# An adaLN, linear-attention and SwiGLU block on one core: a new order for the first scale block, and the output-projection fold in three batches

## The chip, the core and the metric

The kernel runs on one core of one Trainium2 chip. The core has five engines [...]: TensorE (PE, matmuls and 128x128 transposes; its weight loads are listed as PEld), VectorE (DVE), ScalarE (ACT), GpSimd (POOL) and SyncE (SP, which here only issues DMAs). DMAs issued from SP, ACT and POOL share 16 DMA engines. On-chip data lies in SBUF, matmul results in PSUM, which is used here as eight banks of 512 f32 columns: two pools, "pa" and "pb", of four banks each.

The metric is the device time of one execution, in microseconds, as the median over several runs. Before the change it is 829.95 us (8 runs, 829.49 to 830.62).

## The reference

x has 2048 rows of 1024 columns in bf16. Six vectors of 1024 come out of one small product with the condition c.

```python
mod = (silu(c) @ w_mod).reshape(1, 6, 1, -1)
sa, ca, ga, sb, cb, gb = mod[:, 0], ..., mod[:, 5]
h = layernorm(x) * (1 + ca) + sa
x = x + ga * A(h)                      # linear attention, 32 heads of 32
h = layernorm(x) * (1 + cb) + sb
x = x + gb * B(h)                      # (silu(h @ w_gate) * (h @ w_up)) @ w_down, F = 3584

# A(h): q, k, v = h @ wqkv; phi(t) = where(t > 0, t + 1, exp(t)) + 1e-6
kv  = sum_s phi(k)_s v_s               # 32 x 32 for each head
z   = sum_s phi(k)_s
o   = (phi(q) @ kv) / (phi(q) . z + 1e-6)
A   = o @ wo
```

## The kernel before

**Tiling.** The 2048 rows form four chunks (sc) of 512, each of four row tiles of 128. A 1024-wide contraction is eight blocks (cc) of 128. Almost every matmul is 128x128 weights times 512 columns into one PSUM bank. Big tiles (8 KB for each partition: weights, activations, phi(k), v, phi(q)) come from one pool of 19, called k8.

**Loads.** SP issues the first loads in the order of the program: x tiles 0 and 1, the eight blocks of w_mod's first scale columns (wca, 256 KB each; the first of them goes out from ACT), then wv's eight blocks with x tiles 2 and 3 among them, the eight blocks of the shift columns (wsa), the eight of wk, four more x tiles, and wq.

**The start (lines 454 to 529).** The instructions of DVE, ACT and POOL inside `in_order` keep the order in which they are written; PE keeps its program order everywhere. `keep_warm` and `keep_warm_f32` are matmuls on zeros whose result nobody reads. c is turned into a column layout and put through silu (scT). Row tiles 0 and 1 are normalised (xn), transposed on PE (`pe_transpose_tile`) and copied from PSUM to hT by DVE. `mod_rows` makes a row of the modulation on PE: for each of eight blocks j, four matmuls, each on a strip of 32 of the array's columns, stream 256 columns of weights. `mod_turn` then turns the row with a DVE transpose. For the very first column block, one more matmul for each j (`first`) gives the scale as a column right away. hs = hT times the scale; v of chunk 0 is computed from hs (`v_mms`), in groups of one PSUM bank each (row tile t, half nb of the columns), and the shift's part of v is added much later through a correction (vb, KVB). After v, the shift rows are made (`mod_rows(0, ...)`), hT gets scale and shift in place (`modulate_all`), and the k groups of chunk 0 begin, each of eight matmuls that need one wk block each.

**The middle.** For each later chunk: k groups, the kv sums of the chunk before (`kv_phase`: 128 matmuls of 64 columns on 32-column strips), v groups. phi takes an Exp on ACT and two DVE operations for each group. `mod_step` makes the other modulation vectors on DVE, with a broadcast row sc_row of silu(c), which the start builds with eight PE matmuls and two ACT copies. ga is multiplied into wo.

**The fold (lines 590 to 627).** After the last kv sums, kv is folded into wo, so that the attention output is one product of phi(q) with a folded wo. One unit of the fold is (h, nb, g): a PSUM bank that gets four matmuls, i = 0 to 3, each of 32x32 weights times 512 columns on the array tile of row group g and column group i.

```python
for i in range(HPC):
    for g in range(4):
        rs = slice(g * DH, (g + 1) * DH)
        mm(ps[g][i * DH:(i + 1) * DH, :], lhsT=KVT[rs, h, i * DH:(i + 1) * DH], rhs=wo[h][rs, i, ns], ...)
```

There are 16 units, in four batches of four, each batch on the four banks of "pb"; the results go back into wo in place, copied by ACT and DVE in turn. q groups of chunks 1 and 2 stand between the batches.

**The rest.** `wo_tile` applies the folded wo, adds x and normalises; `gate_up` and `down` are the SwiGLU part and take the time from about 200 us on.

Of the kernel before, what the change touches and what calls it, by code (L numbers as in the profile page):

```python
# [21 lines left out]
def kernel(  # L22
# [17 lines left out]
    DH = 32  # L40
# [62 lines left out]
    def big(name, shape):  # L103
        return k8.tile([P] + shape, BF16, name=name, tag="k8")
# [9 lines left out]
    c_sb = const.tile([DC, P], BF16, name="c_sb")  # L114

# [8 lines left out]
    for st in range(2):  # L124
        load_x(st, nc.sync)
# [3 lines left out]
    wca = [big("wme", [4, D]) for _ in range(2)]  # L129
# [6 lines left out]
    for j in range(DC):  # L136
        load_block(wca, wm_v, j, D, nc.scalar if j == 0 else nc.sync)
    for cc in range(DC):
        load_block(wv, wqkv_v, cc, 2 * D)
        if cc in (1, 4):  # L140
            load_x(2 + cc // 4, nc.sync)
# [26 lines left out]
    sc_row = const.tile([P, D], BF16, name="sc_row")  # L168
# [11 lines left out]
    sel = const.tile([P, HPC, P], BF16, name="sel")  # L180
# [17 lines left out]
    def bn(src, mv_out):  # L198
        stats = small.tile([P, NNB, nc.vector.BN_STATS_DIM], F32, name="stats")
        for i in range(NNB):  # L200
            nc.vector.bn_stats(out=stats[:, i, :], in_=src[:, i * NB:(i + 1) * NB])  # L201
        nc.vector.bn_aggr(out=mv_out, in_=stats[:])

    def normalise(dst, src, mean, rstd):
        nc.vector.tensor_scalar(out=dst, in0=src, scalar1=mean, scalar2=rstd, op0=ALU.subtract, op1=ALU.mult)

    def normalise_act(dst, src, mv, rstd):
        nmr = small.tile([P, 1], F32, name="nmr")
        last_nmr[0] = nc.gpsimd.tensor_scalar(out=nmr[:], in0=mv[:, 0, 0:1], scalar1=rstd[:, 0:1], scalar2=-1.0,  # L209
                                op0=ALU.mult, op1=ALU.mult)  # L210
        nc.scalar.activation(out=dst, in_=src, func=ACT.Identity, bias=nmr[:], scale=rstd[:, 0:1])  # L211
# [5 lines left out]
    def pe_transpose_tile(hT, xn, t):  # L217
        tp = acc_b("tp", (DC, P), BF16)
        for cc in range(DC):
            transpose(tp[:, cc, :], xn[:, cc * P:(cc + 1) * P])  # L220
        nc.vector.tensor_copy(out=hT[:, :, t * P:(t + 1) * P], in_=tp[:])
# [3 lines left out]
    def ln1_stats(sc, t):  # L225
        x_sb = x_tiles.pop(sc * STC + t)
        mv = small.tile([P, STC, 2], F32, name="mv")
        bn(x_sb, mv[:, 0, :])
        rstd = rstd_of(mv, 1)
        return sc, t, x_sb, mv, rstd  # L230

    def ln1_norm(sc, t, x_sb, mv, rstd, dve=False):
        xn = k2.tile([P, D], BF16, name="xn", bufs=4)
        if dve:
            normalise(xn[:], x_sb[:], mv[:, 0, 0:1], rstd[:, 0:1])
        else:
            normalise_act(xn[:], x_sb[:], mv, rstd)
        if sc > 0:
            last_load[0] = nc.sync.dma_start_transpose(hTs[sc][:, :, t * P:(t + 1) * P], xn[:])
        return xn  # L240
# [14 lines left out]
    def mod_rows(q, lo, hi, first=None):  # L255
        for j in range(lo, hi):
            if first is not None:
                mm(first, lhsT=wca[j // 4][:, j % 4, 0:P], rhs=scT[:, j:j + 1], start=False, stop=j == DC - 1)
            row_matvec(mod_ps[:, q * MW:(q + 1) * MW], sc32[:, j, :], (wsa, wca)[q][j // 4][:, j % 4, :],
                       q == 0 and j == 0, j == DC - 1)  # L260

    def mod_turn(lo, hi):
        nc.vector.transpose(out=scr_t[:, lo * DH:hi * DH], in_=mod_ps[:, lo * DH:hi * DH])

    def scale_to(hs, hT, cc, lo, hi):
        nc.vector.tensor_scalar(out=hs[:, cc, lo:hi], in0=hT[:, cc, lo:hi], scalar1=ca0T[:, cc:cc + 1], scalar2=None,
                                op0=ALU.mult)

# [185 lines left out]
    nc.vector.memset(sel[:], 0.0)  # L454

    def keep_warm(acc, n):
        for _ in range(n):
            mm(acc[:], lhsT=sel[:, 0, :], rhs=sel[:], start=True, stop=True)

    def keep_warm_f32(acc, n):  # L460
        zeros = sel[:].rearrange("p h n -> p (h n)").bitcast(F32)
        for _ in range(n):
            mm(acc[:, 0:zeros.shape[1]], lhsT=zeros[:, 0:P], rhs=zeros, start=True, stop=True)

    accs = [acc_a() for _ in range(4)]
    spare = accs[3]
    keep_warm_f32(spare, 3)
    keep_warm(spare, 1)
# [5 lines left out]
    with in_order(nc.vector, nc.scalar, nc.gpsimd):  # L474
        mod_ps = acc_b("mod_ps")
        mm(mod_ps[:, 0:DC], lhsT=c_sb[:], rhs=ident[0:DC, 0:DC], start=True, stop=True)
        for g in range(4):
            mm(mod_ps[g * DH:(g + 1) * DH, MW:2 * MW], lhsT=ident[:, 0:DH], rhs=base_t[:, 0:MW], start=True, stop=False)
        nc.scalar.activation(out=scT[:], in_=mod_ps[:, 0:DC], func=ACT.Silu)
        xn0 = ln1_norm(*ln1_stats(0, 0))  # L480
        st1 = ln1_stats(0, 1)
        nc.vector.tensor_copy(out=sc32[:], in_=scT[:].unsqueeze(2).to_broadcast([P, DC, DH]))
        xn1 = ln1_norm(*st1, dve=True)
        keep_warm_f32(spare, 1)
        for h in range(2):
            for j in range(DC // 2):
                mm(accs[h][:, j * P:(j + 1) * P], lhsT=scT[:, 4 * h + j:4 * h + j + 1].to_broadcast([P, P]), rhs=ident[:],
                   start=True, stop=True)
            nc.scalar.copy(out=sc_row[:, h * NB:(h + 1) * NB], in_=accs[h][:])
        keep_warm(spare, 3)  # L490
        first = accs[2][:, 0:1]
        mm(first, lhsT=ident[:], rhs=base_t[:, 0:1], start=True, stop=False)
        mod_rows(1, 0, 3, first)
        pe_transpose_tile(hT, xn0, 0)
        pe_transpose_tile(hT, xn1, 1)
        mod_rows(1, 3, DC, first)
        keep_warm(spare, 1)
        nc.vector.tensor_scalar(out=hs[:, 0, 0:H], in0=hT[:, 0, 0:H], scalar1=first, scalar2=None, op0=ALU.mult)
        mod_turn(DC, 2 * DC)
        for cc in range(1, 4):  # L500
            scale_to(hs, hT, cc, 0, H)
        xn2 = ln1_norm(*ln1_stats(0, 2))
        for cc in range(4, DC):
            scale_to(hs, hT, cc, 0, H)
        st3 = ln1_stats(0, 3)
        gs = k_groups[0:4]
        v_mms(hs, gs, accs, 0, 6)
        pe_transpose_tile(hT, xn2, 2)
        for cc in range(DC):
            scale_to(hs, hT, cc, H, H + P)  # L510
        xn3 = ln1_norm(*st3)
        v_mms(hs, gs, accs, 6, DC)
        gs2, accs2 = k_groups[4:6], [acc_b("acc") for _ in range(2)]
        v_mms(hs, gs2[0:1], accs2[0:1])
        v_evac(0, gs, accs)
        pe_transpose_tile(hT, xn3, 3)
        for cc in range(DC):
            scale_to(hs, hT, cc, H + P, SCW)
        v_mms(hs, gs2[1:2], accs2[1:2])
        mod_rows(0, 0, DC)  # L520
        mod_turn(0, DC)
        nc.vector.tensor_copy(out=sca[:], in_=scr[:, :, :, 0])
        v_evac(0, gs2, accs2)
        for g in k_groups[6:8]:
            acc = acc_a()
            v_mms(hs, [g], [acc])
            v_evac(0, [g], [acc])
        modulate_all(hT, ca1T, saT)
        nc.vector.tensor_copy(out=sc32[:], in_=saT.unsqueeze(2).to_broadcast([P, DC, DH]))
# [3 lines left out]
    for h in range(2):  # L533
        with tc.issue_after(last_load[0].ins):
            nc.sync.dma_start(out=wq[h][:], in_=wqkv_v[:, 4 * h:4 * h + 4, 0:D])
# [5 lines left out]
    for sc in range(NSC):  # L541
        if sc > 0:
            k_phase(sc, 0, 2)
            kv_phase(sc - 1)
            k_phase(sc, 2, 3)
# [45 lines left out]
    q_phase(1, 1, 2)  # L591
# [10 lines left out]
    def fold_wo(h, nb):  # L602
        ns = slice(nb * NB, (nb + 1) * NB)
        ps = [acc_b("wf") for _ in range(4)]
        for i in range(HPC):
            for g in range(4):
                rs = slice(g * DH, (g + 1) * DH)
                mm(ps[g][i * DH:(i + 1) * DH, :], lhsT=KVT[rs, h, i * DH:(i + 1) * DH], rhs=wo[h][rs, i, ns],
                   start=True, stop=True)
        for g in range(4):  # L610
            (nc.scalar.copy if g % 2 == 0 else nc.vector.tensor_copy)(out=wo[h][:, g, ns], in_=ps[g][:])

    q_phase(1, 2, 5)
# [5 lines left out]
    den_sum(0, acc_a())  # L619
    fold_wo(0, 0)  # L620
    den_spread(0)
    q_phase(1, 6, 8)
    fold_wo(0, 1)
    q_phase(2, 0, 2)
    fold_wo(1, 0)
    q_phase(2, 2, 4)
    fold_wo(1, 1)
# [3 lines left out]
    def wo_tile(st):  # L631
# [10 lines left out]
        for nb in range(NNB):  # L642
            ns = slice(nb * NB, (nb + 1) * NB)
            a_ps = acc_b("a_ps")
            for hg in range(HG):
                mm(a_ps[:], lhsT=pq[:, hg, t * P:(t + 1) * P], rhs=wo[hg // 4][:, hg % 4, ns],
                                 start=(hg == 0), stop=(hg == HG - 1))
# [144 lines left out]
```

## Time and profile before

| what | us |
|---|---|
| median of 8 runs | 829.95 |
| lowest and highest | 829.49, 830.62 |
| the profiled execution, its own time | 829.89 |
| span of its profile, first to last instruction | 828.1 |
| first useful matmul (acc<-wv) starts | 11.32 |
| first k group starts | 27.28 |
| fold, first batch to last | 154.82 to 166.96 |
| all HBM reads of the span | 101.98 MB |

The page of the profile gives, for the whole span, the busy time of each engine, the chain of work that ended last (followed back from the last instruction to whatever released each step) and the costliest groups of instructions. A group line reads: source line, engine, operation, output<-inputs, shapes, count, then busy time and mean duration. Nearly every PE instruction carries line 98 or 101, those of the two helpers `mm` and `transpose`, so PE's work is told apart by its tiles. The end of a matmul in the trace is modelled [...]; the pace of PE is read from starts. In the chain and in PE's timeline below, rows of equal instructions are merged.

### The profile page before, as it was taken

The numbers are of one execution on the slowest core, as the hardware profiler recorded it, in microseconds if no ns is written. First come the engines' busy times: TensorE is split into PE (matmuls) and PEld (weight loads), VectorE is DVE, ScalarE is ACT, GpSimd is POOL, SyncE is SP. The second block draws the span as 40 slices with busy tenths as digits, with TensorE's granted clock in tenths as the row PEclk, the third lists the DMA queues.
The fourth block names the chain that finished last, engine by engine and source line by source line (L and its number), as shares of the span: only waits on it lengthen the run. The fifth ranks groups of instructions, "written<-read, shape, count | busy, mean of one in ns | idle before, by whom it ended". The sixth has DMA issues, their size and how long they took to land.

```text
span 828.1 us, 11287 instructions
## 1 busy us (share of the span) xinstructions
PE 822.9 (99%) x4609; PEld 379.1 (46%) x4609; DVE 348.8 (42%) x680; ACT 168.0 (20%) x253; POOL 63.9 (8%) x165
## 2 busy tenths in 40 slices
PE   9999999999999999999999999999999999999998
PEld 5444444444444444444444444444444444444444
DVE  6869778886353344421111354222224432222222
ACT  3545343434111101101111010111111101111000
POOL 2101020120222002000000010000001100000000
PEclk9999999999999999999999999999999999999999
DMA  9978454139995836446252272753405629610011
GB/s 341 307 167 191 117 114 102 44 106 321 366 227 201 251 111 192 140 162 212 91 161 93 63 223 89 251 188 112 143 0 182 149 66 358 220 43 1 19 58 51
DMA packets 142212, 129.07 MB, mean 156 GB/s; under 512 B 58768, under 2 KB 120720, under 8 KB 141648
## 3 DMA queue, kind: packets, MB, share of 16 engines
q1 hardware_dynamic: 138208, 115.10, 46.4%
q0 software_dynamic: 3792, 12.98, 5.1%
q8 instruction: 36, 0.59, 0.3%
q10 hardware_dynamic: 160, 0.26, 0.1%
q14 instruction: 16, 0.13, 0.1%
HBM read 101.98 MB, written 12.72 MB: 138 GB/s over the span
## 4 chain that ended last, share of the span: by engine, by line
PE 98%; DMA 1%; DVE 0%; ACTq 0%; issue 0%
PE acc L98 90%; PE a_ps L98 7%; DMA wme<-in_w_mod_dram 1%; PE kvp L98 1%; PE wf L98 0%; PE den L98 0%; PE mod_ps L98 0%; PE tp L101 0%; PE vb L98 0%; ACTq L126 0%; DVE e L708 0%; DVE ob L711 0%
## 5 line engine op out<-in xcount | busy, mean ns | idle before, releaser
L98 PE MATMUL acc<-h2T,wgu 128*128 128x512 bf16 x1792 | 387.6, 379 | 0.0
L98 PEld LDWEIGHTS <-wgu 128*128 128x128 bf16 x1792 | 175.2, 98 | 211.3
L687 DVE TENSOR_TENSOR gu<-acc,e 128x512 bf16<-128x512 f32 x112 | 77.5, 692 | 289.9 <-PE acc L98 287.1
L98 PE MATMUL acc<-wd,gu 128*128 128x512 bf16 (+2 forms) x924 | 196.1, 373 | 0.0
L686 ACT ACTIVATE e<-acc 128x512 f32<-128x512 f32 x112 | 66.9, 597 | 374.8 <-PE acc L98 374.8
L98 PEld LDWEIGHTS <-gu 128*128 128x128 bf16 x924 | 89.3, 98 | 104.5
L708 DVE TENSOR_TENSOR e<-acc,gb_bc 128x512 f32<-128x512 f32 (+2 forms) x33 | 22.3, 675 | 131.7 <-PE acc L98 128.8
L98 PEld LDWEIGHTS <-hT 128*128 128x128 bf16 x448 | 43.6, 98 | 52.3
L98 PE MATMUL a_ps<-wo,pq 128*128 128x512 bf16 x256 | 57.4, 379 | 0.0
L98 PE MATMUL acc<-hT,wq 128*128 128x512 bf16 x256 | 56.7, 379 | 0.0
L98 PE MATMUL acc<-wk,hT 128*128 128x512 bf16 x256 | 56.4, 379 | 0.0
L273 ACT ACTIVATE eb<-acc 128x512 bf16<-128x512 f32 x64 | 37.6, 594 | 61.4 <-PE acc L98 59.2
L211 ACT ACTIVATE xn<-x,nmr,rstd 128x1024 bf16<-128x1024 f32 x16 | 19.8, 1240 | 126.2 <-POOL nmr L209 125.4
L98 PE MATMUL acc<-wv,hT 128*128 128x512 bf16 x192 | 41.9, 379 | 0.0
L98 PEld LDWEIGHTS <-pq 128*128 128x128 bf16 x256 | 25.1, 98 | 30.2
L655 POOL DMA_DIRECT2D x_scratch<-x x16 | 9.8, 615 | 373.7 <-DVE x L648 373.6
L98 PEld LDWEIGHTS <-wq 128*128 128x128 bf16 x256 | 24.6, 98 | 29.9 <-issue 1.1
L274 DVE TENSOR_SCALAR eb<-eb 128x512 bf16<-128x512 bf16 x64 | 18.3, 290 | 25.8 <-ACT eb L273 25.8
L648 DVE TENSOR_TENSOR x<-a_ps,x_sb 128x512 f32<-128x512 f32 x32 | 22.1, 691 | 8.6 <-PE a_ps L98 8.6
L195 POOL TENSOR_TENSOR rstd<-veps,neg_half 128x1 f32<-128x1 f32 x32 | 17.9, 561 | 99.0 <-DVE veps L193 86.7
L201 DVE BATCH_NORM_STATS2 stats<-x_sb 128x6 f32<-128x512 bf16 x32 | 20.9, 673 | 4.7 <-DMA x_sb<-in_A_x_dram 4.6
L711 DVE TENSOR_TENSOR ob<-e,x1r 128x512 bf16<-128x512 f32 (+2 forms) x33 | 22.3, 675 | 1.0
(99 smaller groups left out, 321.0 us busy)
## 6 DMA issues: line engine op xcount, KB each, us to landing
wgu<-in_B_w_gate_dram SPq DMA_DIRECT2D x28, 1024.0 KB, 6.8
wgu<-in_B_w_up_dram SPq DMA_DIRECT2D x28, 1024.0 KB, 8.0
x_sb<-in_A_x_dram SPq DMA_DIRECT2D x32, 256.0 KB, 5.3
x_scratch<-x POOLq DMA_DIRECT2D x16, 512.0 KB, 3.1
x1r<-x_scratch SPq DMA_DIRECT2D x31, 256.0 KB, 2.9
wd<-in_B_w_down_dram SPq DMA_DIRECT2D x7, 1024.0 KB, 6.8
rbc<-rden_scratch POOLq DMA_DIRECT2D x16, 256.0 KB, 7.6
out_dram<-ob SPq DMA_DIRECT2D x31, 128.0 KB, 1.7
```

What stands on the lines that cost most here:

```text
L98: return tc.keep_in_program_order(nc.tensor.matmul(out, lhsT=lhsT, rhs=rhs, start=start, stop=stop))
L195: nc.gpsimd.tensor_tensor(out=rstd[:, 0:n], in0=veps[:, 0:n], in1=neg_half[:].to_broadcast([P, n]), op=ALU.pow)
L201: nc.vector.bn_stats(out=stats[:, i, :], in_=src[:, i * NB:(i + 1) * NB])
L211: nc.scalar.activation(out=dst, in_=src, func=ACT.Identity, bias=nmr[:], scale=rstd[:, 0:1])
L273: nc.scalar.activation(out=e[:], in_=acc, func=ACT.Exp)
L274: nc.vector.tensor_scalar(out=e[:], in0=e[:], scalar1=1.0, scalar2=PHI_EPS, op0=ALU.min, op1=ALU.add)
L648: nc.vector.tensor_tensor(out=x1[:, ns], in0=a_ps[:], in1=x_t[:, ns], op=ALU.add)
L655: nc.gpsimd.dma_start(out=x1_dram[st * P:(st + 1) * P, :], in_=x1[:])
L686: nc.scalar.activation(out=sg[:], in_=ps[0][:], func=ACT.Silu)
L687: gm = nc.vector.tensor_tensor(out=guT[sc][f // GPT][:, f % GPT, :], in0=ps[1][:], in1=sg[:], op=ALU.mult)
L708: nc.vector.tensor_tensor(out=yt, in0=y_ps, in1=gb_bc[:, ns], op=ALU.mult)
L711: nc.vector.tensor_tensor(out=ob, in0=yt, in1=x1r, op=ALU.add)
```

## The change

At the start, the scale block is loaded in two halves of 512 columns (wca[h] is now [8 blocks, 512 columns], two blocks for each DMA, runs of 1 KB), half 0 ahead of wv and half 1 after wv's first four blocks; x tile 2 is loaded ahead of them. For half 0 the scale is made as four columns by matmuls that stream one column each (`ca_cols`), in four steps with no-op f32 matmuls between them. For half 1 it is made as a row as before, with 128 streamed columns for each matmul (`ca_rows`). Row tiles 0 and 1 are transposed in halves into two PSUM tiles; the first four blocks are scaled from there into hs by DVE, and ACT copies the PSUM tiles to hT. Tile 2's statistics are split around the normalisation of tile 1, which DVE and ACT share. Tile 2 (first four blocks) and tile 3 are scaled straight from PSUM. The v groups run over blocks 0 to 3 first, then 4 to 7. sc_row is no longer built by PE: c's row is loaded, put through silu by ACT, written to DRAM and read back as a broadcast.

Later, kv_phase comes one k group (or q group) earlier, and one q group of chunk 1 comes after it. The fold runs in batches of 5, 6 and 5 units, on "pb" and "pa" banks, into new tiles wof; the sums of den use a "pb" bank.

```diff
-    for st in range(2):
+    for st in range(3):
         load_x(st, nc.sync)
...
-    wca = [big("wme", [4, D]) for _ in range(2)]
+    wca = [big("wme", [DC, NB]) for _ in range(2)]
...
-    for j in range(DC):
-        load_block(wca, wm_v, j, D, nc.scalar if j == 0 else nc.sync)
-    for cc in range(DC):
+    def load_ca(h, eng0):
+        for k in range(4):
+            js = slice(2 * k, 2 * k + 2)
+            (eng0 if k == 0 else nc.sync).dma_start(out=wca[h][:, js, :], in_=wm_v[:, js, D + h * NB:D + (h + 1) * NB])
+
+    load_ca(0, nc.scalar)
+    nc.scalar.dma_start(out=sc_row[0:1, :], in_=c)
+    for cc in range(4):
         load_block(wv, wqkv_v, cc, 2 * D)
-        if cc in (1, 4):
-            load_x(2 + cc // 4, nc.sync)
+    load_ca(1, nc.sync)
+    load_x(3, nc.sync)
+    for cc in range(4, DC):
+        load_block(wv, wqkv_v, cc, 2 * D)
...
+    def ca_rows():
+        mod_rows(lambda j: wca[1][:, j, :], DC + 4, 4)
...
+    def scale_turned(tp, cc, t):
+        nc.vector.tensor_scalar(out=hs[:, cc, t * P:(t + 1) * P], in0=tp[:, cc, :], scalar1=ca0T[:, cc:cc + 1],
+                                scalar2=None, op0=ALU.mult)
...
+    def keep_warm(*widths):
+        for n in widths:
+            mm(accs[3][:, 0:n], lhsT=zeros[:, 0:P], rhs=zeros[:, 0:n], start=True, stop=True)
...
+        def ca_cols(k):
+            for i in range(4):
+                for j in (2 * k, 2 * k + 1):
+                    mm(cols[i], lhsT=wca[0][:, j, i * P:(i + 1) * P], rhs=scT[:, j:j + 1], start=False,
+                       stop=j == DC - 1 and i in (0, 3))
...
+        keep_warm(NB)
+        ca_cols(0)
+        keep_warm(NB, 2 * P)
+        ca_cols(1)
+        turn_half(xn0, 0, 0)
+        ca_cols(2)
+        keep_warm(P)
+        turn_half(xn0, 0, 1)
+        turn_half(xn1, 1, 0)
+        ca_cols(3)
+        keep_warm(P)
...
+        scale_first(0)
+        next(bn2)
+        rstd2 = rstd_of(mv2, 1)
+        for cc in range(1, 4):
+            scale_first(cc)
...
+        v_mms(hs, gs, accs, 0, 1)
+        turn_half(xn1, 1, 1)
+        nc.scalar.copy(out=hT[:, 4:8, 0:H], in_=tps[1][:])
+        nc.scalar.activation(out=sc_row[0:1, :], in_=sc_row[0:1, :], func=ACT.Silu)
+        v_mms(hs, gs, accs, 1, 3)
+        tp2 = turn_tile(xn2)
+        for cc in range(4):
+            scale_turned(tp2, cc, 2)
+        nc.scalar.copy(out=hT[:, :, H:H + P], in_=tp2[:])
+        v_mms(hs, gs, accs, 3, 4)
+        ca_rows()
+        mod_turn(DC + 4, 2 * DC)
...
+    nc.gpsimd.dma_start(out=sc_dram[:], in_=sc_row[0:1, :])
+    with tc.issue_after(wq_load.ins):
+        nc.sync.dma_start(out=sc_row[:], in_=sc_dram[:].to_broadcast([P, D]))
...
-            k_phase(sc, 0, 2)
+            k_phase(sc, 0, 1)
             kv_phase(sc - 1)
-            k_phase(sc, 2, 3)
+            k_phase(sc, 1, 3)
...
-    def fold_wo(h, nb):
-        ns = slice(nb * NB, (nb + 1) * NB)
-        ps = [acc_b("wf") for _ in range(4)]
+    wof = [big("wof", [4, D]) for _ in range(2)]
+    fold_units = [(h, nb, g) for h in range(2) for nb in range(NNB) for g in range(4)]
+
+    def fold_wo(accs):
+        units = [(fold_units.pop(0), acc) for acc in accs]
         for i in range(HPC):
-            for g in range(4):
+            for (h, nb, g), acc in units:
                 rs = slice(g * DH, (g + 1) * DH)
-                mm(ps[g][i * DH:(i + 1) * DH, :], lhsT=KVT[rs, h, i * DH:(i + 1) * DH], rhs=wo[h][rs, i, ns],
-                   start=True, stop=True)
-        for g in range(4):
-            (nc.scalar.copy if g % 2 == 0 else nc.vector.tensor_copy)(out=wo[h][:, g, ns], in_=ps[g][:])
-
-    q_phase(1, 2, 5)
+                mm(acc[i * DH:(i + 1) * DH, :], lhsT=KVT[rs, h, i * DH:(i + 1) * DH],
+                   rhs=wo[h][rs, i, nb * NB:(nb + 1) * NB], start=True, stop=True)
+        for k, ((h, nb, g), acc) in enumerate(units):
+            (nc.scalar.copy if k % 2 == 0 else nc.vector.tensor_copy)(out=wof[h][:, g, nb * NB:(nb + 1) * NB], in_=acc[:])
+
+    q_phase(1, 1, 5)
...
-    den_sum(0, acc_a())
-    fold_wo(0, 0)
+    den_sum(0)
+    fold_wo([acc_b("wf") for _ in range(3)] + [acc_a() for _ in range(2)])
     den_spread(0)
     q_phase(1, 6, 8)
-    fold_wo(0, 1)
-    q_phase(2, 0, 2)
-    fold_wo(1, 0)
-    q_phase(2, 2, 4)
-    fold_wo(1, 1)
+    q_phase(2, 0, 1)
+    fold_wo([acc_b("wf") for _ in range(4)] + [acc_a() for _ in range(2)])
+    q_phase(2, 1, 4)
+    fold_wo([acc_b("wf") for _ in range(4)] + [acc_a()])
```

## The prediction

> **What bounds the kernel now.** I read four views, in this order. First the page, for the engine that sets the end.
>
> ```profile
> PE 822.9 (99%) x4609; PEld 379.1 (46%) x4609; DVE 348.8 (42%) x680; ACT 168.0 (20%) x253; POOL 63.9 (8%) x165
> ...
> PE 98%; DMA 1%; DVE 0%; ACTq 0%; issue 0%
> ```
>
> TensorE (PE) is busy for 99% of the span and holds 98% of the chain that ended last. A microsecond is therefore gained or lost only where PE waits or streams something useless, or where its matmuls are fewer or come in a worse order. Next the chain of waits in the first 30 us (start, length, what).
>
> ```profile
> 1.33 3.58 DMA wme<-in_w_mod_dram
> 4.91 0.02 issue
> 4.92 5.55 DMA wme<-in_w_mod_dram
> 10.47 0.05 issue
> 10.52 0.18 PE acc L98
> 10.70 0.22 PE mod_ps L98 x4
> 10.92 0.32 PE acc L98
> 11.24 0.08 issue
> 11.32 1.89 PE acc L98 x8
> ```
>
> The first useful matmul starts at 11.32. It waits for the last of the ten 256 KB blocks (x tiles 0 and 1, eight of the scale block) that the transfers deliver by 10.47. From there on the chain is PE alone. This is the wait that the change attacks, so the next question is whether those transfers only come in the wrong order or are themselves the bound. For that I took busy time in two stretches (PE, PEld, DVE, ACT, POOL, granted clock, DMA share, GB/s) and the rows of the tile wk.
>
> ```profile
> 8.00:28.00 20.00, 19.70 (x162) 10.15 (x159) 14.76 (x49) 7.07 (x12) 3.32 (x39) 1.00 1.05 394
> 194.00:204.00 10.00, 10.00 (x48) 4.55 (x47) 7.81 (x19) 4.66 (x7) 0.00 (x0) 1.00 1.08 369
> ...
> L98 PE MATMUL acc<-wk,hT x36: 379/379/379, 27.3 to 34.8; 128*128 128x512 bf16 x36
> L134 SPq DMA_DIRECT2D wk<-in_A_wqkv_dram x8: 327/328/328, 18.5 to 23.3; - x8
> ...
> DMA to landing us min/median/max: 5.4/5.4/5.4
> ```
>
> From 8 to 28 us the DMA engines are full (share 1.05) at 394 GB/s. The last wk block is issued at 23.26 and lands 5.36 later, at 28.62. The first k group starts at 27.28 and its eighth matmul, which needs that block, comes seven spacings of 0.2157 us later, at 28.79. So the load stream is only 0.17 us ahead of PE at this point. Last, PE's timeline around the fold:
>
> ```profile
> 153.31 1.03 PE L98 MATMUL acc<-hT,wq 128*128 128x512 bf16 x4
> 154.26 0.63 PE L98 MATMUL acc<-pq,Zden 128*32 128x128 bf16 x32
> 154.82 0.43 PE L98 MATMUL wf<-wo,kvs 32*32 32x512 bf16 x16
> 155.19 3.63 PE L98 MATMUL acc<-hT,wq 128*128 128x512 bf16 x16
> 158.75 0.43 PE L98 MATMUL wf<-wo,kvs 32*32 32x512 bf16 x16
> 159.12 0.60 PE L98 MATMUL acc<-hT,wq 128*128 128x512 bf16 x2
> ```
>
> Sixteen fold matmuls, one on each 32x32 tile of the array, take 0.37 us from the first start to the next full-array start (154.82 to 155.19). A single one streams 512 columns, 0.213 us at the spacing above, so all sixteen run at once.
>
> [...] sixteen tiles overlap here; no run yet shows a matmul for a free tile held behind one for a busy tile. [...] from the last q matmul before a fold to the fold is 0.31 us against a spacing of 0.216, so 0.09 us. [...] The 256 KB blocks do land one after another, 0.66 us apart. [...] The f32 no-ops here are 0.427 us apart before 4.4 us and faster after it[...].
>
> **The change, part by part.**
>
> *Start.* The ten blocks before the first useful matmul become seven (x tiles 0 to 2, four of scale half 0), and wv's first block is the eighth. With 0.665 us a block, the seventh lands at 10.47 - 3 x 0.665 = 8.47. The scale halves move 1 KB runs instead of 2 KB. The second stretch above, mostly FFN weights in 1 KB runs, gives 369 GB/s against 394: 4 blocks cost 0.18 more, all eight 0.36. So scale half 0 is there at 8.65, the first hs piece (a 0.29 us DVE row, L498, now read from PSUM) near 9.3, wv's first block at 9.35, and the first useful matmul at about 9.4, 1.9 us earlier.
>
> *From there to the k groups.* PE owes 64 v matmuls (13.8 us), 20 transposes at 0.056 (1.1; it was 16 in the kernel before, whose other 16 came ahead of the start), the scale rows of half 1 (32 of 128 columns, about 0.65 with both mode changes) and the shift rows (1.0, the 0.99 of 22.90). Half 1 is the fifteenth block: 10.47 + 5 x 0.665 + 0.36 = 14.15. PE is at its rows after 16 matmuls and 12 transposes, 9.4 + 3.45 + 0.67 = 13.5, and waits 0.65. Sum: 9.4 + 13.8 + 1.1 + 0.65 + 1.0 + 0.65 = 26.6, against 27.28 before. The early start has shrunk to 0.7.
>
> *The k groups.* The transfers in front of the last wk block are the same blocks in another order, plus the 0.36 for the shorter runs; one 2 KB row of c is added on ACT's queue. So that block lands at 28.62 + 0.36 = 28.98, its matmul goes at 29.03, and the second group starts at 29.25. Before, it started at 27.28 + 8 x 0.2157 = 29.01. The whole start comes out at **+0.25 us**: PE reaches the k groups earlier and waits for wk there. Bounds: the 1 KB price may be nothing, and an instruction fetch (36 packets, 0.59 MB on the page, so 16 KB each) [...] can move by its own length, near 0.8 us (SP's longest wait for wv). That gives -0.4, where PE's own 26.6 + 1.73 rules again, to +0.7. Work moved to ACT (hT copies, scale copies) and DVE (scaling from PSUM) lies beside those matmuls. If it slipped, it would first use up the 0.6 us that PE waits for wk.
>
> *No-ops.* sel's five f32 and bf16 groups give way to f32 ones of 512, 256 and 128 columns between the steps. They run while PE waits for blocks: nothing. [...]
>
> *kv one group earlier, q tile 1 later, sc_row by a DMA round trip.* The same matmuls and mode changes in another order. v's last copy ends 0.6 us after its matmul and kv still has a k group (1.73 us) of cover. sc_row's read-back stands on SP behind wq and ahead of the hT transposes, which are needed only near 57 us: nothing.
>
> *Fold.* Before: 4 batches x 0.37 plus 4 mode changes x 0.09 = 1.84 us. After: batches of 5, 6 and 5 units. A unit is four matmuls, i = 0..3, on tiles (g, i), and the loop has i outside and units inside. In each batch two units share a g. For every i the fifth matmul therefore meets a tile that is still streaming, waits 0.213, and holds everything behind it. First to last start is 3 x 0.22 + 0.216 = 0.87 instead of 0.05, so a batch takes 0.37 + 0.82 = 1.19. Three of them plus 3 x 0.09 = 3.84 us, **+2.0 us**. Bounds: if a held matmul let those for other tiles pass, a tile would have two turns per batch, 0.58 a batch and 2.0 in all, +0.2. [...] 12 x 0.09 more, +3.1. I take +2.0, [...] because matmuls that follow each other on the same tile keep one stream length apart: den's 96, four tiles of 128 columns at a time, take 1.45 us of the chain, 0.060 for each four, where 128 columns stream in 0.054. The copies to wof (16 of 0.6 to 0.68 us, as before) stay beside q matmuls; the two "pa" accumulators per batch come back before q needs them, three groups later. Every later stage is PE without gaps, so this reaches the end.
>
> Sum: +0.25 + 2.0 = +2.25 us on the profiled execution's span of 828.1. Its own time is 829.89 (1.8 around the span, untouched), and the median of the runs 829.95 is 0.06 above it. Forecast: **832.2 us**.
>
> **Rivals.**
> A. Forecast as above, 832.2, chance 0.72.
> B. Tiles dispatch independently: the fold costs +0.2, total +0.45, 830.4. For: tiles overlap freely at 0.003 us in the trace. [...] 0.13.
> C. Not slower but faster: the start's 1.9 us reach the end, the wk stream running ahead as soon as PE's order allows, and the fold as in B: 829.95 - 1.9 + 0.2 = 828.3. It decides if the last wk block lands before 27.1 instead of 29.0. Against: the full DMA share from 8 to 28 us, and PE's own sum of 26.6. 0.07.
> D. Slower still: [...] near 833.3. 0.08.
>
> **How the numbers follow.** The likeliest is A. The range 830.2 to 833.4 takes in B, D and A with the start at either bound (831.5 to 832.7); only C lies outside. What a measurement can tell from no change is about 0.2%, 1.66 us. A is beyond that unless the start is at its best bound, so slower is 0.67 of A's 0.72 plus D, 0.75. Same is B plus the rest of A, 0.18. Faster is C, 0.07.
>
> **What would show it.** Start: first acc<-wv near 9.4, a PE wait of 0.5 to 0.8 us for wme near 13.5, first acc<-wk near 26.6 with a wait for wk in it, second k group at 29.2 or 29.3. Fold: three wf batches of about 1.2 us each. The prediction is wrong if a batch takes 0.6 or less, or if the second k group starts before 28.5.

## The result, and the profile after

The changed kernel takes 833.18 us (median of 10 runs, 831.94 to 834.77), the kernel before beside it 829.89: ratio 1.0040, 95% interval 1.0032 to 1.0048. That is about 3.3 us slower, where the forecast was 2.25 us slower. The profiled execution took 834.58 with a span of 832.8, so 4.7 us more than the 828.1 of the kernel before. The page, for the engine that sets the end:

```profile
PE 824.9 (99%) x4623; PEld 378.9 (46%) x4623; DVE 347.0 (42%) x684; ACT 173.7 (21%) x261; POOL 65.1 (8%) x167
...
PE 96%; DMA 3%; issue 0%; SPq 0%; DVE 0%
```

TensorE still sets the end, and its share of the chain fell from 98 to 96% because the chain now runs through transfers for longer at the start. The chain of waits of the changed kernel, its end within the first 40 us (start, length, what):

```profile
23.66 5.36 DMA wk<-in_A_wqkv_dram
29.02 0.04 issue
29.06 10.95 PE acc L98 x50
```

The last wk block lands at 29.02 (forecast 28.98) and its matmul goes at 29.06, so the second k group starts one spacing of 0.216 later, near 29.27 (forecast 29.25, before 29.01). The start does what the forecast said. Next the fold, on the timeline of PE:

```profile
159.48 0.39 PE L98 MATMUL wf<-wo,kvs 32*32 32x512 bf16 x3
159.49 0.38 PE L98 MATMUL acc<-wo,kvs 32*32 32x512 bf16 x1
159.50 0.39 PE L98 MATMUL wf<-wo,kvs 32*32 32x512 bf16 x3
159.51 0.39 PE L98 MATMUL acc<-wo,kvs 32*32 32x512 bf16 x1
159.51 0.39 PE L98 MATMUL wf<-wo,kvs 32*32 32x512 bf16 x3
159.53 0.38 PE L98 MATMUL acc<-wo,kvs 32*32 32x512 bf16 x1
159.53 0.39 PE L98 MATMUL wf<-wo,kvs 32*32 32x512 bf16 x3
159.54 0.59 PE L98 MATMUL acc<-wo,kvs 32*32 32x512 bf16 x5
160.06 5.35 PE L98 MATMUL acc<-hT,wq 128*128 128x512 bf16 x24
```

In the program, each step i has five matmuls: three on wf, two on acc, of which the second acc one needs the tile that the first wf one occupies. Yet after one acc matmul the next step's wf matmuls start at once. The four that conflict come at the end, inside the last row with its five. A batch takes 0.58 us from first start to the next q matmul, not the 1.19 of the forecast. So the forecast's main term did not occur. What did is in the chain of the changed kernel from 50 to 70 us, a place that the forecast had passed over:

```profile
49.94 7.12 PE acc L98 x33
57.06 1.15 PE kvp L98 x128
58.21 1.19 PE acc L98 x5
59.40 2.54 issue
61.94 8.11 PE acc L98 x29
```

"issue" means that PE waits for nothing that the profile shows. It stands still for 2.54 us in the middle of a k group, and no operand is named as missing. Busy times around it (start:end, length, then PE, PEld, DVE, ACT, POOL, granted clock, DMA share, GB/s):

```profile
59.40:61.94 2.54, 0.00 (x0) 0.00 (x0) 0.00 (x0) 0.00 (x0) 0.00 (x0) 1.00 0.08 17
...
62.91:66.32 3.41, 3.41 (x10) 1.21 (x8) 0.98 (x2) 0.87 (x2) 0.00 (x0) 0.50 0.03 5
66.32:70.00 3.68, 3.68 (x18) 1.67 (x17) 3.38 (x9) 1.14 (x3) 0.00 (x0) 1.00 0.23 53
```

All five stand still at once, and 0.97 us after PE resumes the granted clock falls to 0.50 for 3.41 us. Half of 3.41 makes another 1.7 us, an estimate. The 2.54 count from a modelled end; by starts (59.02 to 61.94, less one spacing) PE loses 2.70. The sum closes nearly: second k group +0.26, stall 2.70, clock 1.7, fold 0.2 make 4.9, against 4.7 between the two spans and 4.85 between the starts of the last matmul.

What does PE wait for? The page of either kernel has 36 packets of 16 KB on a queue called "instruction". PE's 4609 matmuls and 4609 weight loads on the page make 256 for each packet, the 4623 of each in the changed kernel 257. In the records, fetches come on average 254.5 and 253.0 PE instructions apart. So a block, as the text below calls it, is one packet of about 256 PE instructions, an estimate from these counts. Two stretches of the changed kernel's DMA queues (queue, kind: packets, MB, and the time of the packets as a share of 16 engines, which can pass 100% where packets overlap), 54.0 to 59.4 and then 59.4 to 60.6:

```profile
q1 hardware_dynamic: 5576, 1.42, 116.2%
```

```profile
q1 hardware_dynamic: 129, 0.03, 10.9%
q8 instruction: 1, 0.02, 5.5%
```

Before 59.4 the DMA engines are full (116.2%), with w_mod's transposing loads (wmt). The fetch starts only at 59.46, when these run out; PE goes on 2.48 us later. In the kernel before, the fetch starts at 57.87, just as the same loads run out there, and PE is not yet dry. Its queues from 57.8 to 59.0:

```profile
q8 instruction: 1, 0.02, 5.0%
q1 hardware_dynamic: 22, 0.00, 1.7%
```

The loads run later in the changed kernel because SP issues them later. SP's timeline of the kernel before, then of the changed one (the starts count; the merged last row ends with the view):

```profile
34.31 9.50 SPq L239 DMA_TRANSPOSE hT<-xn  x4
43.91 1.96 SPq L121 DMA_DIRECT2D x_sb<-in_A_x_dram  x4
45.92 21.41 SPq L380 DMA_TRANSPOSE wmt<-in_w_mod_dram  x3
```

```profile
36.28 9.76 SPq L247 DMA_TRANSPOSE hT<-xn  x4
46.14 1.96 SPq L123 DMA_DIRECT2D x_sb<-in_A_x_dram  x4
48.15 9.88 SPq L392 DMA_TRANSPOSE wmt<-in_w_mod_dram  x2
```

The hT transposes start 2 us later and push the x loads and wmt by 2.2. They wait for chunk 1's xn, whose first tile ACT starts at 35.02 instead of 33.05. On DVE the modulation of chunk 0, now 16 half rows, ends at 29.8 instead of 27.3. Before, DVE then waited for x until 29.34, so chunk 1's statistics start only 0.58 later, at 29.92. The larger part comes next: the phi work of the first two k groups (31.11 to 33.3) now runs ahead of the step that sums up the first tile's statistics, at 33.23 instead of 31.14.

This is the theory (T) that the runs had to test. PE's next block of instructions is itself a DMA, and behind queued loads it comes late. A rival (R) puts the loss into the new scale block or its order on DVE. T needs a second piece: kv_phase is 128 matmuls and 128 weight loads, by the estimate above a whole block, that PE uses up in 1.15 us, where 128 full-size matmuls take 27.6 (at 0.216). Around kv_phase, T says, PE therefore has almost no stock to wait with.

### The profile page after: what moved, and what is told of

The parts are those of the page before. It is cut to its first block, busy times and chain, and to the rows that moved or that the text cites. A ratio compares the mean times of both kernels' runs of the same rounds, so it can differ in the third digit from the quotient of the medians.

```text
span 832.8 us, 11335 instructions
## 1 busy us (share of the span) xinstructions
PE 824.9 (99%) x4623; PEld 378.9 (46%) x4623; DVE 347.0 (42%) x684; ACT 173.7 (21%) x261; POOL 65.1 (8%) x167
## 4 chain that ended last, share of the span: by engine, by line
PE 96%; DMA 3%; issue 0%; SPq 0%; DVE 0%
PE acc L98 88%; PE a_ps L98 7%; DMA wme<-in_w_mod_dram 1%; DMA wv<-in_A_wqkv_dram 1%; DMA wk<-in_A_wqkv_dram 1%; DMA x_sb<-in_A_x_dram 1%; PE kvp L98 1%; PE den L98 0%; PE wf L98 0%; PE vb L98 0%; SPq L123 0%; DVE e L757 0%; DVE ob L760 0%; PE tp L101 0%
## 5 line engine op out<-in xcount | busy, mean ns | idle before, releaser
L98 PE MATMUL acc<-wk,hT 128*128 128x512 bf16 x256 | 58.7, 387 | 3.1 <-issue 2.5
L98 PE MATMUL a_ps<-wof,pq 128*128 128x512 bf16 x256 | 57.4, 379 | 0.0
L221 ACT ACTIVATE xn<-x_sb,nmr,rstd 128x1024 bf16<-128x1024 bf16 (+1 forms) x17 | 19.6, 1163 | 15.3 <-POOL nmr L216 12.2
```

What stands on the lines that cost most here:

```text
L98: return tc.keep_in_program_order(nc.tensor.matmul(out, lhsT=lhsT, rhs=rhs, start=start, stop=stop))
L221: nc.scalar.activation(out=dst[:, ws], in_=src[:, ws], func=ACT.Identity, bias=nmr[:], scale=rstd[:, 0:1])
```

## The experiments

The numbers give the order of the runs, and each ratio is to the kernel before as it ran beside them: a median of 830.11 for e1 to e4, 829.99 for e5 to e8, 830.14 for e9 and e10, 829.98 for e11 and e12.

### One part of the change alone

**e2_before_kv_early**: the kernel before with only kv_phase moved.

```diff
-            k_phase(sc, 0, 2)
+            k_phase(sc, 0, 1)
             kv_phase(sc - 1)
-            k_phase(sc, 2, 3)
+            k_phase(sc, 1, 3)
```

(and q tile 1 behind kv, as in the change).

> The kernel before with nothing changed but kv_phase one group earlier. T: the transposing loads end at 57.8 as in the kernel before, instructions come at about 60.3, PE's stock ends near 59.2: a stall of about 1.1 us, 831.0. R2: the stall of the changed kernel, 2.7 us and perhaps a clock dip: 832.5 or more. If the fetch has nothing to do with it: 829.9.

830.20, ratio 1.0003 (0.9995 to 1.0011). The move costs nothing by itself. T had said 831.0, a miss: the loads ran out at 56.8 and not at 57.8, the fetch started there, at 56.84, and PE had no gap but one of 0.16 us behind kvp.

**e3_before_fold3**: the kernel before with only the fold in three batches of 5, 6 and 5 units.

```diff
-    fold_wo(0, 0)
+    fold_wo([acc_b("wf") for _ in range(3)] + [acc_a() for _ in range(2)])
...
-    fold_wo(0, 1)
-    q_phase(2, 0, 2)
-    fold_wo(1, 0)
-    q_phase(2, 2, 4)
-    fold_wo(1, 1)
+    q_phase(2, 0, 1)
+    fold_wo([acc_b("wf") for _ in range(4)] + [acc_a() for _ in range(2)])
+    q_phase(2, 1, 4)
+    fold_wo([acc_b("wf") for _ in range(4)] + [acc_a()])
```

> The kernel before with the fold alone in three batches of 5, 6 and 5 units into wof. As recorded in the forecast (a held matmul holds all behind it): batches of 1.2 us, 831.9. Rival, each tile takes its next matmul when it is free: batches of 0.58 us, 830.1.

830.48, ratio 1.0006 (0.9997 to 1.0014). Its second batch on PE's timeline:

```profile
161.08 0.46 PE L98 MATMUL wf<-wo,kvs 32*32 32x512 bf16 x16
161.30 0.44 PE L98 MATMUL acc<-wo,kvs 32*32 32x512 bf16 x8
161.67 5.35 PE L98 MATMUL acc<-hT,wq 128*128 128x512 bf16 x23
```

From 161.08 to 161.67 it takes 0.59 us. The interval leaves no room for +2.0 us (0.24%): the fold's forecast term falls.

### One part of the change undone

**e1_after_kv_back**: the changed kernel with kv_phase back behind two k groups.

```diff
-            k_phase(sc, 0, 1)
+            k_phase(sc, 0, 2)
             kv_phase(sc - 1)
-            k_phase(sc, 1, 3)
+            k_phase(sc, 2, 3)
```

(and q tile 1 ahead of the last kv sums, as in the kernel before).

> The changed kernel with kv_phase moved back behind two k (or q) groups; head and fold as changed. Theory T: PE's instruction list is itself fetched by a DMA, the fetch that is wanted near 57 us is held until the transposing loads of w_mod (wmt) are through at about 59.4, and PE gets its next instructions some 2.5 us after that, near 61.9. With kv back, PE's stock would last to about 59.9, so a stall of about 2 us remains: 832 to 833.5. Rival R2, the move of kv alone makes PE outrun its instructions: the stall is gone, 830.2 to 830.6. Rival F, the fold costs 2 us by itself: without the stall 832.2.

831.93, ratio 1.0028 (1.0019 to 1.0037), just under T's 832 to 833.5. Its chain of waits:

```profile
58.67 1.20 PE kvp L98 x125
59.86 1.17 issue
61.03 0.21 PE kvp L98 x3
```

The stall is there, 1.17 instead of 2.54, and now inside kvp, three matmuls before its end. In the changed kernel PE got five k matmuls beyond kvp. Moving kv back put eight matmuls of a k group ahead of it, and eight is the shift: PE stops at the same place in its list of instructions, not at the same piece of work. That speaks for the end of a block. The fetch started at 58.53, and PE resumed 2.50 later. It did not wait for the loads to end, though: they ran at a DMA share of 1.27 just before it (57.5 to 58.5) and went on until 61.5; a lull lay about 2 us back.

**e4_after_turned_first**: the changed kernel with the transposing loads ahead of the x loads of chunk 2.

```diff
+        if sc == 0:
+            with tc.issue_after(last_load[0].ins):
+                last_load[0] = mod_load(2, gaT)
         if sc + 2 < NSC:
             for st in range((sc + 2) * STC, (sc + 3) * STC):
```

> The changed kernel with the transposing loads of w_mod's columns for gaT issued ahead of the four x tiles of chunk 2 instead of behind them. T: they are through about 2 us earlier, near 57.4, instructions come near 59.9, PE's stock ends at 59.2: a stall of about 0.7 us and no clock dip, 831.0. R2: stall and dip as before this edit, 832 to 834.8.

831.90, ratio 1.0025 (1.0015 to 1.0036); T had said 831.0. The transposing loads are through near 56.3, but the fetch starts at 59.12, when most of the x loads behind them are through. So it isn't the transposing alone: here the fetch came late behind ordinary loads, with the queue of loads at 95.0% of the 16 engines from 56.3 to 59.0. The chain:

```profile
58.80 1.03 PE acc L98 x4
59.82 1.58 issue
61.40 8.79 PE acc L98 x40
```

### The instructions shifted against the work

If the end of a block is what matters, then instructions without use, put into PE's idle time of the start, must move the stall.

**e8_after_80_more** and **e10_after_80_dense**: the changed kernel with 40 matmuls (80 instructions with their weight loads) in place of one of the no-ops; of one column in e8, of 64 in e10.

```diff
-        keep_warm(NB, 2 * P)
+        keep_warm(2 * P)
+        for _ in range(40):
+            mm(accs[3][:, 0:64], lhsT=ident[:], rhs=ident[:, 0:64], start=True, stop=True)
```

> The changed kernel with 40 one-column matmuls (80 PE instructions) in place of one of the start's idle-time matmuls of 0.93 us. T: the fetch that was late is asked for 80 instructions earlier, near 45 us, when no long loads are queued, and the following one is asked for inside kvp with a whole block in hand: no stall near 59 us, 830.4 to 830.6, that is, more instructions make it faster. R: 833.2 as without them.

830.35, ratio 1.0011 (1.0004 to 1.0017). In its profile, of an execution of 832.4, there was no stall near 59 us, but PE's records were long from 4.8 us on, ahead of the added matmuls, until 13.9 (the two no-ops at 4.8 span 2.06 us, in the changed kernel 1.14), and the first useful matmul came at 12.1. Six of the 21 runs lie at 832.4 to 832.6. Whether matmuls of one column prolong the slow start isn't shown; e10 took 64 columns instead:

> As e8_after_80_more, but each of the 40 added matmuls has 64 columns instead of one, so that PE is not thinly used in the idle time of the start (in the profile of e8_after_80_more the first useful matmul came at 12.1 us instead of 9.6 and the records were longer up to there). T: the start is as in the changed kernel (first useful matmul near 9.6, second k group near 29.3), the fetch is asked for near 45 to 50 us, no stall near 59 us: 830.4 with a span near 828.6. R: the stall near 59 us stays, 832 to 834.8.

830.38, ratio 1.0005 (0.9997 to 1.0013), span 828.4. The chain of e10, and its fetch in the stretch from 47.3 to 48.5:

```profile
49.94 7.12 PE acc L98 x33
57.06 1.15 PE kvp L98 x128
58.21 11.98 PE acc L98 x55
```

```profile
q1 hardware_dynamic: 139, 0.24, 65.0%
q8 instruction: 1, 0.02, 12.6%
```

From 49.94 to 58.21 this is the changed kernel to the hundredth. But by T PE has the block already, fetched at 47.34 between two groups of loads, and nothing stops. Chunk 1's first v matmul starts at 70.24 instead of 74.64: the 4.40 are the 2.70 of the stall and the 1.70 of the clock. The 40 useless matmuls make the changed kernel 2.8 us faster (833.18 against 830.38; the kernel before ran at 829.89 and 830.14 beside them). With the no-op gone the trace has 38 weight loads more, so 76 instructions. The scale block and its order on DVE are unchanged, so R has nothing left to explain.

### The loads moved, or the cause put into the kernel before

**e6_after_late_turn**: the changed kernel with the transposing loads behind kv_phase(0).

```diff
             if sc == 1:
+                mod_load(2, gaT, True)
                 mod_load(3, sbT, True)
...
-        if sc == 0:
-            with tc.issue_after(last_load[0].ins):
-                last_load[0] = mod_load(2, gaT)
```

> The changed kernel with the two transposing loads of w_mod for gaT issued in chunk 1 behind kv_phase(0) instead of at the end of chunk 0. T: no load is queued when PE wants its next instructions (about 55 to 57 us), so the fetch starts there, no stall near 59 us and no clock drop behind it; what remains of the change is the start's +0.25 and the fold's +0.2: 830.4 to 830.6. R: the stall near 59 us stays, 832 to 834.8.

837.45, ratio 1.0088 (1.0075 to 1.0102): a miss in the time. With no load under way the fetch started at 56.74, against 59.46 in the changed kernel, whose PE has as many instructions ahead of that place, and the stall near 59 us was gone, as T said. But the late loads pushed chunk 2's hT transposes behind them on SP, and PE stood still for 4.04 us until 88.47. The chain:

```profile
84.76 3.12 DMA hT<-xn
...
88.00 0.42 DVE hT L224
88.43 0.05 issue
88.47 3.58 PE acc L98 x8
```

**e5_before_pad** and **e9_before_pad_behind**: the kernel before with an unread 1 MB load, ahead of the two transposing loads in e5, behind them in e9.

```diff
+            pad = big("pad", [4, D])
+            with tc.issue_after(last_load[0].ins):
+                last_load[0] = nc.sync.dma_start(out=pad[:], in_=wqkv_v[:, 0:4, 0:D])
```

> The kernel before with one extra 1 MB load that nobody reads, queued between the x loads of chunk 2 and the two transposing loads of w_mod, so that the queue of loads empties about 2.6 us later (it was at 57.9 us). Theory T (PE's next 16 KB of instructions is itself a DMA that waits behind the loads already queued; PE resumes 2.5 us after the fetch starts): PE wants the block from about 57 us, the fetch starts near 60.4 instead of 57.87, PE can go on near 62.9, while its stock ends near 61.2 (kvp's end at 59.6 and some 7 matmuls); a stall of about 1.7 us, near 831.8. Rival R (the loss of the changed kernel comes from its new scale block or its order on DVE, not from instruction supply): no stall near 60 us, 830.1.

830.25, ratio 1.0004 (0.9996 to 1.0012): a miss. The fetch started at 59.07, early enough. The expectation for e9 below puts that into a gap between the two transposing loads. The trace has this gap at 56.4 to 57.0 (DMA share 0.17); at 58.5 to 59.0 the share is 1.22 again, so the fetch came in about 2 us behind the gap, with the second load in full stream.

> The kernel before with the extra 1 MB load that nobody reads queued behind the two transposing loads of w_mod, so that no gap is left between them in which PE's instructions could slip through, as they did at 59.07 us in e5_before_pad. T: the fetch wanted near 57 us starts when the pad is nearly through, 59.5 to 60.4 us; PE can go on 2.4 us later, at 62 to 62.8; its stock ends some 8 matmuls behind kvp, near 61.3: a stall of 0.7 to 1.5 us near 61 us, 830.7 to 831.6. Rival R (instruction supply plays no part): no stall, 830.0.

830.05, ratio 0.9998 (0.9990 to 1.0007). PE's timeline of e9, and its queues in the stretches from 57.2 to 60.4 and from 60.4 to 61.4:

```profile
58.73 1.22 PE L98 MATMUL kvp<-v,pk 128*32 128x64 bf16 x128
59.88 2.55 PE L98 MATMUL acc<-wk,hT 128*128 128x512 bf16 x11
62.86 4.49 PE L98 MATMUL acc<-wk,hT 128*128 128x512 bf16 x20 [0.43 <-issue]
```

```profile
q1 hardware_dynamic: 498, 0.99, 87.1%
```

```profile
q8 instruction: 1, 0.02, 6.0%
q1 hardware_dynamic: 2, 0.00, 0.1%
```

The fetch started at 60.44, with the pad through, and PE resumed 2.42 later. So the kernel before has the same stall once its loads last longer. It is 0.43 us instead of the expected 0.7 to 1.5, since PE got 11 matmuls beyond kvp and not 8. That is too little for the timed runs to show: their 830.05 is what R said, and the stall is seen in the profile alone.

**e7_before_32_more**, **e11_before_46_more**, **e12_before_46_more_and_pad**: the kernel before with more instructions at the start: 16 one-column matmuls in e7 (32 instructions), the edit below in e11 and e12 (46 by my count; the trace has 21 weight loads more, so 42), and in e12 e9's pad as well.

```diff
-    keep_warm_f32(spare, 3)
-    keep_warm(spare, 1)
+    keep_warm_f32(spare, 2)
+    for _ in range(24):
+        mm(spare[:, 0:64], lhsT=sel[:, 0, :], rhs=sel[:, 0, 0:64], start=True, stop=True)
```

> The kernel before with 16 more one-column matmuls (32 PE instructions with their weight loads, about 0.4 us) in PE's idle time before c arrives at 4.48 us. T: the block of instructions that PE lacks begins 32 instructions earlier against the work, in the last part of kvp: PE's stock ends near 59.5 instead of 61.2, the fetch still starts at 57.9 and PE resumes near 60.4: a stall of about 0.9 us, 831.0. R: 830.1.

> The kernel before with 24 matmuls of 64 columns in PE's idle time of the start, in place of two of the matmuls without use there: 46 PE instructions more ahead of kvp, PE as busy as before in that time. In e9_before_pad_behind the stock ended 11 matmuls behind kvp, near 62.3; with 46 instructions more it ends inside kvp, near 59.5. T: the fetch starts when the transposing loads are through, at 56.8 to 57.9, and PE can go on at 59.2 to 60.3: no stall or one of up to 0.8 us, 830.1 to 830.9. R: 830.1.

> Both additions to the kernel before at once: the 46 PE instructions of e11_before_46_more and the unread 1 MB load behind the transposing loads of e9_before_pad_behind, which cost nothing measurable each by itself. T: the stock ends near 59.5 inside kvp, the fetch starts near 60.4 behind the pad and PE goes on near 62.8: a stall of about 3.3 us inside kvp, and perhaps the drop of the granted clock behind it (1.7 us more): 833.4 to 835.2. R (the two are independent and instruction supply plays no part): 830.1 to 830.3.

831.00 (ratio 1.0010, 1.0003 to 1.0017), 830.62 (1.0008, 1.0000 to 1.0016) and 830.46 (1.0005, 0.9997 to 1.0014). e7 gave the expected time for another reason: no stall, but the k groups started 1.1 us later. In e11 and e12 the fetch started as early as 53.25 and 54.11: in e11 in the lull between the two transposing loads, in e12 about 1 us behind it, with the second one in full stream (share 1.27 from 53.5 to 54.1). So a stall of over 3 us, put into the kernel before, was not achieved. That an early request escapes agrees with T, but e12's time lies nearer to R's 830.1 to 830.3 than to T's 833.4 and shows nothing against R.

## Why the prediction was right and wrong

The direction and the range held, the mechanism did not: the largest term did not come, and a somewhat larger loss, from steps that the prediction had put at nothing, stood in its place. Step by step:

**Start: right.** First useful matmul at 9.60 (forecast 9.4), first k group at 26.53 (26.6), last wk block at 29.02 (28.98), second k group at 29.27 (29.25): +0.26 for +0.25. The early start is eaten by the load stream, as worked out. One term on the way did not come: PE did not wait 0.65 for the second scale half. Its rows began at 13.82, 0.31 behind the matmul before, the same step as at 23.8 (0.31). So 26.53 fits 26.6 in part by luck; the last wk block, which sets the end of this stretch, does not depend on it.

**Fold: wrong, +0.2 instead of +2.0.** The step "waits 0.213, and holds everything behind it" (the measured spacing is 0.216) failed in its second half. In the records of the batch above a matmul for a busy tile held only its own tile: sixteen matmuls start between 159.48 and 159.54 and the four that conflict at 159.71 to 159.76, each 0.226 behind the one on its tile, and after later ones of the program. That PE keeps its program order everywhere, as said of the kernel before, is thus not true of these starts. I had written that no run yet showed a matmul for a free tile held behind one for a busy tile, and then let that holding, my assumption, carry 0.72 of the chance. That was rival B's mechanism, at 0.13. (In the batch of six, two pairs of units share a g, and not one; either sum stays as it is.)

**"kv one group earlier ... nothing": wrong.** The step listed hT's transposes as "needed only near 57 us". It asked when the work needs their result, and not what is behind them on SP. They came 2 us later, so the loads behind them did too, and behind these PE's next instructions. The prediction knew of instruction fetches only as something that may move a load. Compared with the kernel before, three shifts meet. The fetch starts 1.59 later (57.87 to 59.46). kvp starts 1.47 earlier (58.46 to 56.99). And the block ends six matmuls earlier behind kvp (5 against the 11 that e9 showed for the kernel before), 1.3 us. Before, by this estimate, PE would have run dry near 62.2 and could have gone on near 60.3 (57.87 + 2.45), 1.9 us in hand. That less 4.4 is the stall of 2.5.

**The sum.** 2.25 was forecast as 0.25 + 2.0. It is 0.25 + 0.2, which e10 confirms within its error once the stall is gone (830.38), plus the stall. Behind it the clock dropped in the profiled run: it and two more of the ten, at 834.3 to 834.8, have a mean granted clock of 0.998; the other seven, at 0.999 or 1.0, are at 831.9 to 833.9. That the range held the time was chance, and so was a slowdown that stands clear of noise: 0.45 alone would not have.

Left open: which part of the new scale block delays hT (the sixteen half rows and the new order of phi and statistics on DVE are the likeliest, but neither was undone alone); why the seven runs at 0.999 or 1.0 spread over 2 us, as one execution alone was profiled; and what exactly the fetch waits for. It need not be the end of the loads or an idle moment, since in e1, e5 and e12 it started with the engines full (DMA share 1.27, 1.22 and 1.27). No version beat the kernel before: what remains of the change without the stall is the start's and the fold's small losses.

## What to carry to other kernels

When every engine stands still and the chain says "issue", look at the instruction packets. Here one started behind full loads at 59.46, and PE, which had stood still since 59.40, went on 2.48 us after that start. A stretch of small matmuls like kvp, which by the estimate above used up a block in 1.15 us, is the place to look at first, where the next packet starts behind a long stretch of queued loads. Of a step that is moved, follow what stands behind it on its queue to the end, also where its own result has time. An order of starts that the trace has not yet shown is a hypothesis with two prices, not the likeliest case.

## What the runs showed of the hardware

- A packet of 16 KB on the instruction queue took 0.88 to 1.18 us near 53 to 61 us, and 1.87 (e8) and 2.41 (e10) with loads starting beside it. PE resumed 2.28 to 2.50 us after its start (changed kernel 2.48, e1 2.50, e4 2.28, e9 2.42). No wait in the profile names it.
- With no load under way this packet started at 56.74 (e6), behind full loads at 59.46 (changed kernel) and 60.44 (e9). In e1, e5 and e12 it started 1 to 2 us behind a lull, with the DMA share at 1.2 or more just before it.
- Behind a stall of 2.54 us the granted clock fell to 0.50 for 3.41 us in the profiled execution; behind e6's wait of 4.04 it did so too, for 3.41 from 88.53. The profiles of e1 and e4, with stalls of 1.17 and 1.58, show no drop.
- In the changed kernel's first fold batch, matmuls on 32x32 tiles started out of program order where an earlier one waited for its own tile (159.48 to 159.54 for sixteen, 159.71 to 159.76 for the four that waited).
